# Attention scores in four 64x64 tiles at a time, keys in token order, and a new order of the whole program

## The chip, the cores and the metric

The kernel runs on one core of a Trainium2 chip. The core has five engines that work side by side: TensorE (PE in the profile, its weight loads PEld), VectorE (DVE), ScalarE (ACT), GpSimd (POOL) and SyncE (SP, which here only starts transfers). They share the on-chip memory SBUF; TensorE writes to the eight banks of PSUM. Transfers run on 16 DMA engines. The metric is the time of one execution on the device in microseconds (us).

## What is computed

Cosine attention over 8 batches, 12 heads, 448 tokens and 64 features for each head, and then a highway layer over the 3584 tokens of 768 features:

```python
q_n = q / (np.linalg.norm(q, axis=-1, keepdims=True) + 1e-06)
k_n = k / (np.linalg.norm(k, axis=-1, keepdims=True) + 1e-06)
scores = np.matmul(q_n, k_n.transpose(0, 1, 3, 2)) / tau
attn = np.exp(scores - np.max(scores, axis=-1, keepdims=True))
attn = attn / (np.sum(attn, axis=-1, keepdims=True) + 1e-09)
x = np.matmul(attn, v)                    # then heads side by side: 3584 x 768
H = np.maximum(x @ w_h, 0.0)
T = 1.0 / (1.0 + np.exp(-(x @ w_t + b_t)))
out = T * H + (1.0 - T) * x
```

## The kernel before

**Tokens.** The 448 tokens of a head are read as 64 partitions times 7 pieces: token 7l+j lies in partition l, piece j. Two heads that follow each other lie in the two halves of the partitions (s = 0 and 1), and two such pairs stand side by side (t = 0 and 1). So the program handles "quads" of four heads, three for each batch (g), each of two steps s; a step works on two heads, t = 0 and 1. For each batch there are six steps (p = 0 to 5), 48 in all.

**Stages of a batch.** `ld_qk` and `ld_v` load q, k and v. `norm` squares (ACT, a few on POOL) and sums (DVE, L391), `lnexp` or `newton` turns the sums into reciprocal norms, `scale` multiplies q and k by them (L432, nearly all on POOL), `turn` transposes the result so that features lie on the partitions (PE and a copy by DVE at L462, or a transposing DMA from SP for q from batch 3 and for k from batch 5 on), `scores` makes the products of keys and queries with the keys on the partitions (L496 and L507), ACT takes their exponential into E and Et (L502, L509), `attend` multiplies by v (L521, L526, L534), where a column of ones beside v gives the sum of the row, and DVE divides (L541, L542). Batch 0 does this in smaller pieces in `attend0` (L573 to L629). `ffn` is the highway layer of 112 to 128 tokens at a time, 32 pieces: the transposed x (xT) times w_t and w_h (L682; L679 for the last seventh of the tokens), then bias, tanh, gate and the output on DVE, ACT and POOL (L711 to L762).

**Scores before.** 448 keys are 3 x 128 + 64. For a step, three operations `qk` (L496) each hold two matmuls of 64 x 128 weights, one for each head t in its half of the rows of the array; the two run at the same time. The fourth, `qkt` (L507), takes the last 64 keys of both heads in one matmul of 128 x 128 weights. For it `scale` writes k into eight pieces instead of seven, with zeros where the other head's features stand (L432 in two parts of 4 and 3 pieces; zeros by `zkn`, L281), `turn` transposes eight pieces, and `attend` multiplies Et by two blocks of v at once (L521, 130 columns).

**Order.** Nothing is scheduled while it is built: `ORDER` is a table that says in which order the 1948 operations are issued, `SLOTS` says which buffer each takes; both are written out as numbers. Every engine follows its own queue in that order and waits where data or a buffer is missing. Two rules add waits of their own (the last lines of the kernel): a load of q waits for the ACT operation before it in the order, and a POOL operation waits for the last DVE operation before it where both belong to the kinds in `PORT` (48 such waits).

**Zero products.** 18 + 39 matmuls of a block of zeros (wz, L301 and L305), `WARM` and `NF`, stand between the first real ones. Nothing reads what they make.

Of the kernel before, what the change touches and what calls it, by code (L numbers as in the profile page):

```python
# [20 lines left out]
66 1 67 342 68 0 69 3 72 71 7 70 5 42 61 339 23 19 75 74 64 21 44 52 20 51 22 55 79 9 83 43 2 6 14 13 81 82 73 80 8 85  # L21
86 16 84 15 63 39 341 87 76 88 12 95 96 60 108 25 33 56 31 11 38 24 107 46 89 40 114 113 17 37 109 32 4 90 53 30 111
10 97 18 112 98 93 115 118 110 353 54 116 174 91 137 124 117 94 357 92 29 142 173 175 28 122 105 123 99 340 177 59 119
180 354 121 100 125 120 133 127 128 349 141 126 48 138 26 34 350 154 58 178 347 129 140 153 176 131 578 139 144 143
358 78 134 132 130 106 150 149 45 179 348 155 101 102 343 152 151 156 47 77 186 355 57 359 135 189 181 190 182 192 191
351 360 136 361 50 362 183 146 62 104 103 363 364 145 41 147 36 365 148 184 185 187 27 352 383 198 188 158 162 356 377
378 579 161 165 166 157 35 167 164 159 193 194 163 202 49 382 201 345 168 381 379 169 197 195 196 203 204 209 170 160
206 200 199 212 380 210 171 222 172 346 221 205 384 207 266 234 226 208 267 344 211 224 225 233 223 227 366 367 213
809 214 235 286 271 272 385 368 287 369 370 584 215 371 372 581 592 216 236 228 268 291 217 386 269 238 218 404 585
219 387 245 270 237 273 588 593 248 220 246 229 403 393 240 239 292 430 230 288 247 416 388 242 231 398 293 65 389 432  # L30
241 392 391 394 583 397 289 589 232 243 279 280 413 274 417 431 290 244 427 306 275 281 429 395 428 307 249 415 410
414 316 317 412 250 396 252 390 586 318 594 401 424 253 587 276 580 582 590 402 450 254 376 277 425 311 255 595 312
278 256 808 260 426 259 411 319 451 294 262 591 375 433 261 1263 373 596 434 251 320 374 407 313 597 295 408 263 441
598 264 599 813 409 257 435 600 436 442 308 309 443 437 812 824 816 299 282 601 602 321 265 310 811 438 447 449 258
607 461 448 611 608 444 825 613 634 300 399 301 418 420 463 446 445 462 439 440 467 609 400 421 458 468 464 419 817
631 460 466 405 614 633 465 296 406 297 459 610 612 621 298 818 326 475 617 481 632 476 483 477 455 422 484 423 454
624 327 615 623 616 478 622 469 618 470 819 485 482 501 453 604 479 480 452 502 498 1036 456 302 500 495 619 472 471
487 499 496 492 486 663 488 603 820 620 606 497 605 494 457 473 489 283 637 640 474 490 491 493 814 815 641 505 625
504 503 642 822 638 639 506 643 507 328 508 528 645 329 646 821 509 626 333 334 644 657 647 304 284 303 664 674 330
628 823 335 651 627 648 650 697 680 649 658 566 547 654 826 659 676 681 675 652 660 532 314 827 810 828 829 1038 662  # L40
331 305 830 834 529 315 1037 1039 831 322 332 530 533 832 336 635 531 1035 655 636 843 698 661 513 656 534 1051 514
677 653 1270 671 323 510 511 540 665 337 541 667 678 515 679 629 512 672 673 837 1052 838 666 542 839 842 840 1043 691
685 859 630 855 1044 668 846 847 850 714 518 669 519 520 516 692 715 856 693 683 682 670 848 535 708 688 694 684 537
1271 538 695 1262 689 710 690 686 521 522 539 728 696 687 709 730 705 711 324 841 1045 712 523 567 707 702 713 568 729
833 536 543 1046 569 706 844 1047 701 731 700 338 551 699 732 703 835 851 725 1041 845 722 552 723 724 1048 553 718
559 560 716 717 544 887 726 870 1042 727 1049 889 704 736 719 735 734 890 852 857 733 720 561 721 325 849 285 858 737
556 557 836 860 738 864 872 871 891 888 777 867 861 558 1050 884 570 869 853 885 1274 572 573 886 854 545 865 866 881
898 571 883 1053 739 1054 517 873 758 874 1266 1055 1056 882 862 1057 1058 868 1490 1060 1059 548 863 549 924 900 899
550 892 894 877 876 1067 796 901 904 574 1275 895 878 740 893 1268 1065 1076 546 1087 1264 875 575 879 896 741 903 902
925 524 743 576 907 762 905 1272 526 1278 525 742 897 880 744 770 906 554 918 1279 915 555 908 771 763 916 759 527  # L50
1276 745 1040 1273 1064 760 1073 917 764 1070 1074 748 761 919 920 772 749 1066 1075 932 1082 1505 921 938 751 752 934
933 767 909 940 1083 750 910 941 911 1267 1269 1084 768 958 922 923 939 765 753 1277 935 959 562 769 1062 952 912 1280
766 936 929 797 1068 1063 1078 1489 798 913 914 953 937 746 955 949 577 1069 942 928 951 799 1061 781 782 1281 956 957
773 1265 954 950 563 1071 778 779 1072 926 774 927 1501 780 946 963 783 1111 1108 1282 943 945 1100 944 962 1493 564
# [809 lines left out]
```

## Time and profile before

| what | us |
|---|---|
| median of 3 runs | 255.94 |
| lowest and highest run | 255.06, 262.05 |
| span of the profiled execution, first to last instruction | 252.9 |
| busy in it: PE | 237.5 |
| ACT | 211.5 |
| DVE | 208.0 |
| POOL | 184.0 |

The profile is of one execution and gives its span; a time of the runs also holds what lies around the span, and the profile does not show the device time of that same execution. Between the span and the median of the runs lie 3.0 us. Engines work side by side, so their busy times do not add up. A busy time is that of the union of the instructions; matmuls overlap, and the time from the start of one to the start of the next tells what it costs the queue.

### The profile page before, as it was taken

What the parts mean: (1) busy time and instruction counts of PE and PEld (TensorE: products, weight loads), DVE (VectorE), ACT (ScalarE), POOL (GpSimd) and SP (SyncE); (2) the same over time, 40 slices, a digit from 0 to 9 for tenths busy, and PEclk for the clock granted to TensorE, in tenths of its full rate; (3) what the DMA queues carried; (4) which work ended last, traced back from release to release, by engine and by line L of the source; (5) the groups of instructions that cost most, each with busy time, mean ns of one, the idle gap of its engine ahead of it and who ended that gap; (6) DMA issues with size and microseconds to landing.
All of it is one profiled execution on the core that took longest, in us unless ns stands there. A gap on an engine that the chain in (4) does not pass through costs nothing.

```text
span 252.9 us, 7457 instructions
## 1 busy us (share of the span) xinstructions
PE 237.5 (94%) x2895; PEld 147.1 (58%) x2895; DVE 208.0 (82%) x462; ACT 211.5 (84%) x421; POOL 184.0 (73%) x261
## 2 busy tenths in 40 slices
PE   5959999999999999989999999999999999999990
PEld 2425776557756665645765566656656655675650
DVE  4977989999999999989899869689767665556983
ACT  3589999999999999989999999999997669981120
POOL 8369599959798979796989775878476983522540
PEclk9997999999999999999999999999999999999998
DMA  6999999999589999999999998999779588745755
GB/s 219 286 270 237 288 259 202 200 271 179 72 104 146 314 264 248 151 223 163 266 157 170 156 114 138 249 207 193 128 129 231 93 135 192 162 127 123 187 147 156
DMA packets 75892, 47.78 MB, mean 189 GB/s; under 512 B 51536, under 2 KB 72656, under 8 KB 75856
## 3 DMA queue, kind: packets, MB, share of 16 engines
q1 hardware_dynamic: 55568, 33.86, 59.2%
q0 software_dynamic: 19856, 12.68, 37.1%
q10 hardware_dynamic: 432, 0.75, 0.8%
q8 instruction: 22, 0.36, 0.6%
q14 instruction: 14, 0.11, 0.1%
HBM read 38.34 MB, written 11.01 MB: 195 GB/s over the span
## 4 chain that ended last, share of the span: by engine, by line
PE 68%; DMA 11%; ACT 8%; DVE 7%; issue 2%; POOL 2%; SPq 0%; DVEq 0%; POOLq 0%; ACTq 0%
PE B L682 26%; PE B L496 10%; PE B L526 8%; DMA xT<-x 7%; PE B L679 5%; PE B L521 3%; DMA E<-in_k_dram 3%; PE B L447 3%; ACT E L502 3%; PE B L534 3%; PE B L507 2%; PE B L573 2%; ACT sq L380 2%; PE B L305 2%; DVE hm L720 1%
## 5 line engine op out<-in xcount | busy, mean ns | idle before, releaser
L502 ACT ACTIVATE E<-B 128x448 f16<-128x448 f32 x252 | 122.8, 612 | 9.6 <-PE B L496 8.6
L682 PEld LDWEIGHTS <-xT 128*128 128x128 f16 x576 | 52.1, 98 | 39.6 <-issue 6.9
L752 POOL TENSOR_TENSOR os<-x,hm 128x384 f32<-128x384 f16 x53 | 47.6, 912 | 29.8 <-DVE hm L747 21.3
L682 PE MATMUL B<-wh,xT 128*128 128x384 f16 x288 | 56.7, 326 | 0.6 <-DMA xT<-x 0.6
L682 PE MATMUL B<-wt,xT 128*128 128x384 f16 x288 | 55.0, 326 | 1.8 <-DMA xT<-x 1.4
L432 POOL TENSOR_TENSOR kn<-kr,y 128x192 f16<-128x192 f16 (+1 forms) x84 | 45.8, 562 | 10.6 <-DVE y L409 6.1
L391 DVE TENSOR_REDUCE n<-sq 128x14 f32<-128x896 f32 (+1 forms) x50 | 51.2, 1039 | 2.8 <-ACT sq L380 2.6
L432 POOL TENSOR_TENSOR qn<-qr,y 128x448 f16<-128x448 f32 x47 | 43.9, 946 | 9.1 <-ACT y L420 4.4
L526 PE MATMUL B<-vp,E 128*128 128x65 f16 x756 | 38.7, 193 | 0.0
L724 ACT ACTIVATE tt<-z 128x768 f16<-128x768 f32 (+1 forms) x32 | 26.3, 821 | 14.6 <-DVE z L711 14.5
L720 DVE SCALAR_TENSOR_TENSOR hm<-B,x 128x384 f16<-128x384 f32 x53 | 28.8, 549 | 8.4 <-PE B L682 3.9
L526 PEld LDWEIGHTS <-E 128*128 128x128 f16 x756 | 33.7, 98 | 3.2
L496 PE MATMUL B<-qT,kT 64*128 64x448 f16 x252 | 34.8, 354 | 0.4 <-DVE hm L720 0.4
L711 DVE TENSOR_TENSOR z<-B,bias 128x384 f32<-128x384 f32 x48 | 25.8, 551 | 9.3 <-PE B L682 6.3
L521 PE MATMUL B<-vp,Et 128*128 128x130 f16 x126 | 28.1, 223 | 0.0
L380 ACT ACTIVATE sq<-qr 128x896 f32<-128x896 f32 (+1 forms) x24 | 24.1, 1022 | 3.5 <-DMA qr<-in_q_dram 3.5
L509 ACT ACTIVATE Et<-B 128x448 f16<-128x448 f32 x42 | 26.1, 631 | 0.4 <-PE B L507 0.4
L542 DVE SCALAR_TENSOR_TENSOR x<-B,rd 128x448 f16<-128x448 f32 x42 | 25.6, 618 | 0.9
L337 POOL DMA_DIRECT2D vr<-in_v_dram x32 | 21.9, 690 | 2.5 <-DVE z L711 2.5
L586 ACT ACTIVATE E<-B 128x512 f16<-128x512 f32 (+1 forms) x42 | 20.6, 607 | 0.9 <-POOL qn L432 0.5
L380 ACT ACTIVATE sq<-kr 128x896 f32<-128x896 f16 x17 | 17.0, 1041 | 1.1 <-DMA kr<-in_k_dram 1.1
L305 PE MATMUL B<-wz 128*128 128x512 f16 x39 | 14.7, 433 | 2.6 <-DVE wz L281 2.6
(81 smaller groups left out, 313.7 us busy)
## 6 DMA issues: line engine op xcount, KB each, us to landing
out_dram<-os SPq DMA_DIRECT2D x47, 192.0 KB, 3.3
qr<-in_q_dram SPq DMA_DIRECT2D x6, 1344.0 KB, 8.3
kr<-in_k_dram POOLq DMA_DIRECT2D x7, 672.0 KB, 11.6
vr<-in_v_dram POOLq DMA_DIRECT2D x16, 192.0 KB, 6.9
qr<-in_q_dram SPq DMA_DIRECT2D x6, 448.0 KB, 10.0
vr<-in_v_dram POOLq DMA_DIRECT2D x16, 144.0 KB, 7.7
out_dram<-os SPq DMA_DIRECT2D x15, 96.0 KB, 3.8
wt<-in_moe_w_t_dram POOLq DMA_DIRECT2D x1, 1152.0 KB, 24.4
```

Source lines behind the costliest of these rows:

```text
L380: nc.scalar.activation(dst, src, AF.Square, scale=sc)
L391: nc.vector.reduce_sum(R("n2", b)[:, c : c + 7 * n], a, axis=AX.X)
L432: ENG[eng].tensor_mul(N[:, :, t, :] if nm == "q" else N[:, lo > 0 : (lo > 0) + 2 * (hi - lo) - 1 : 2, t, :], source(nm, b, g)[:, t, 64 * l ...
L496: nc.tensor.matmul(R("B", ("S", n, c, t))[:, 0:S], lhsT=R("kT", i)[ln, s, 128 * c : 128 * c + 128], rhs=queries(ln), start=True, stop=True)
L502: nc.scalar.activation(R("E", n)[:, at : at + 7, :].rearrange("l j x -> l (j x)"), R("B", ("S", n, c, t))[:, 0:S], AF.Exp)
L509: op("ACT", f"expt {n}", lambda: nc.scalar.activation(R("Et", n).rearrange("l j x -> l (j x)"), R("B", ("St", n))[:, 0:S], AF.Exp), r=[("B ...
L521: nc.tensor.matmul(U[:, 2 * c : 2 * c + 2, :], lhsT=Et[:, 2 * c : 2 * c + 2, :].rearrange("l j x -> l (j x)"), rhs=vp[:, 6:8, 0:65], start ...
L526: nc.tensor.matmul(U[:, 2 * c + t, :], lhsT=E[:, at : at + 2, :].rearrange("l j x -> l (j x)"), rhs=vp[:, 3 * t + m, 0:65], start=False, s ...
L682: nc.tensor.matmul(P[:, 0:MH], lhsT=xT[:, cc, :], rhs=w_[:, cc, MH * mh : MH * mh + MH], start=(cc == 0), stop=(cc == CC - 1))
L720: op("DVE", f"hm {g} {mh}", lambda at=at, sl=sl, mh=mh: nc.vector.scalar_tensor_tensor(out=R("hm", g)[:, sl], in0=R("B", at)[:, 0:MH], sca ...
L724: op("ACT", f"th{nb} {g}", lambda: nc.scalar.activation(R("tt", g)[:, 0:W], R("z", g)[:, 0:W], AF.Tanh, scale=0.5), r=[("z", g), ("t0",)], ...
L752: op(eng, f"out {g} {mh}", lambda sl=sl, mh=mh: ENG[eng].tensor_add(R("os", g)[:, sl], xpart(mh), R("hm", g)[:, sl]), r=[("gg", g), xk], w ...
```

## The change

- **Scores in 64x64 tiles.** `score` issues four matmuls of 64 x 64 weights: rows t and columns h of the array are halves, so four tiles. Three operations `qk` for a step take 2 x 64 keys each for two heads, as before. The last 64 keys of the two steps of a quad go together into one operation (`tails`, 21 instead of 42), whose columns h are the two steps. Et then holds both steps in its two halves, one tile for each t, and there are two exponentials for each quad instead of one for each step: 42 as before.
- **k in token order.** k has seven pieces without zeros, like q: `scale` writes it in one operation, `turn` transposes seven pieces, and the transposing DMA is one of 128 partitions instead of two of 64. `zkn` goes. qT and kT have the same layout.
- **Products with v.** The 130 columns of L521 become two matmuls of 65 columns, with zeros in the half of v that belongs to the other step; v is loaded by s instead of by t.
- **Loads.** q is loaded in thirds in all batches (24 transfers instead of 12), and the first k through ACT's queue alone.
- **Batch 0.** q and k of all three quads are scaled half on DVE, half on POOL, instead of that of the first quad alone.
- **Waits.** The two rules go. `BEHIND` is a table of 52 waits: 42 of POOL operations for a DVE operation, 10 of loads of q for an ACT operation.
- **Zero products.** 50 instead of 39 in `NF`, and 18 as before.
- **Order.** `ORDER` and `SLOTS` are new throughout.

```diff
-66 1 67 342 68 0 69 3 72 71 7 70 5 42 61 339 23 19 75 74 64 21 44 52 20 51 22 55 79 9 83 43 2 6 14 13 81 82 73 80 8 85
+74 75 81 4 3 22 0 76 20 82 8 78 5 17 1 9 2 12 77 11 335 19 15 16 10 21 83 18 14 13 80 7 6 23 338 24 87 89 25 26 79 84
...
+BEHIND = dict(
+    map(int, n.split(":"))
+    for n in """
+116:119 136:131 277:589 317:813 332:99 374:358 379:365 547:1250 548:731 564:221 576:275 597:588 732:951 752:1033
...
-    WARM, NF, NLATE = 18, 39, 2
+    WARM, NF, NLATE = 18, 50, 2
...
-    SCALE = {("q", 0, 0): ("DVE", "POOL"), ("k", 0, 0): ("DVE", "POOL")}
+    SCALE = {(nm, 0, g): ("DVE", "POOL") for nm in "qk" for g in range(NG)}
...
+    def score(out, o, w, K, Q, s, c):
+        for t, h in ((0, 0), (1, 1), (0, 1), (1, 0)):
+            ln = slice(64 * t, 64 * t + 64)
+            S_, j = (s, c + h * (4 - s)) if c < NC else (h, 3 + 3 * h)
+            nc.tensor.matmul(out[t][64 * h : 64 * h + 64, o[t] : o[t] + w], lhsT=K[ln, j, S_, :], rhs=Q[ln, :, S_, :], start=True, stop=True)
...
-                for t in range(2):
-                    ln = slice(64 * t, 64 * t + 64)
-                    nc.tensor.matmul(R("B", ("S", n, c, t))[:, 0:S], lhsT=R("kT", i)[ln, s, 128 * c : 128 * c + 128],
-                                     rhs=queries(ln), start=True, stop=True)
-            op("PE", f"qk {n} {c}", fn, r=[tn("q", i), tn("k", i)], w=[("B", ("S", n, c, 0)), ("B", ("S", n, c, 1))], mode="T")
+                score([R("B", ("S", n, c, t)) for t in range(2)], (0, 0), S, R("kT", i), R("qT", i), s, c)
+            op("PE", f"qk {n} {c}", fn, r=[tn("q", i), tn("k", i)], w=[("B", ("S", n, c, 0)), ("B", ("S", n, c, 1))], mode="Q")
...
+    def tails(b, g):
+        i = 3 * b + g
+
         def ft():
-            nc.tensor.matmul(R("B", ("St", n))[:, 0:S], lhsT=R("kT", i)[:, s, 384:512], rhs=queries(slice(0, 128)), start=True, stop=True)
-        op("PE", f"qkt {n}", ft, r=[tn("q", i), tn("k", i)], w=[("B", ("St", n))], mode="F")
+            score([R("B", ("St", i, t)) for t in range(2)], (0, 0), S, R("kT", i), R("qT", i), 0, NC)
+        op("PE", f"qkt {i}", ft, r=[tn("q", i), tn("k", i)], w=[("B", ("St", i, 0)), ("B", ("St", i, 1))], mode="Q")
...
         def full(c):
-            nc.tensor.matmul(U[:, 2 * c : 2 * c + 2, :], lhsT=Et[:, 2 * c : 2 * c + 2, :].rearrange("l j x -> l (j x)"),
-                             rhs=vp[:, 6:8, 0:65], start=True, stop=False)
             for t in range(2):
-                for m in range(NC):
+                for m in range(NC + 1):
+                    lt = E[:, 7 * (2 * m + t) + 2 * c :][:, 0:2] if m < NC else R("Et", (i, t))[:, 2 * c : 2 * c + 2]
+                    nc.tensor.matmul(U[:, 2 * c + t, :], lhsT=lt.rearrange("l j x -> l (j x)"),
+                                     rhs=vp[:, 3 * t + m if m < NC else 6 + t, 0:65], start=(m == 0), stop=(m == NC))
...
-            before = act = None
+            last = {}
...
+                last[o.seq] = made[-1]
+                if o.seq in BEHIND:
+                    behind(made[0], last[BEHIND[o.seq]])
```

What the new order does is best seen in the engines' queues. Rows name the line in the kernel, the instruction, and what it writes and reads. First TensorE in the middle of the program, at the scores of a step. Before, two row pairs of 64x128 tiles and the last keys as one full matmul, and then transposes of k:

```order
L496 LDWEIGHTS kT1_91
L496 MATMUL B3_124<-qT1_87,kT1_91 128x448
L496 LDWEIGHTS kT1_91
L496 MATMUL B5_126<-qT1_87,kT1_91 128x448
L507 LDWEIGHTS kT0_90
L507 MATMUL B0_121<-qT3_89,kT0_90 128x448
L447 LDWEIGHTS kn1_67
L447 MATMUL B7_128<-ident_129,kn1_67 128x2x64
```

And TensorE now, at the last keys of the two steps of a quad, with the highway layer behind them:

```order
L458 LDWEIGHTS kT0_90
L458 MATMUL B7_129<-qT1_87,kT0_90 64x448
L458 LDWEIGHTS kT0_90
L458 MATMUL B4_126<-qT1_87,kT0_90 64x448
L458 LDWEIGHTS kT0_90
L458 MATMUL B7_129<-qT1_87,kT0_90 64x448
L458 LDWEIGHTS kT0_90
L458 MATMUL B4_126<-qT1_87,kT0_90 64x448
L665 LDWEIGHTS xT0_106
L665 MATMUL B3_125<-wt_132,xT0_106 128x384
```

Four matmuls of half the partitions, two into each of two banks, stand where one full matmul stood, once for two steps. Counted along TensorE's whole queue, neighbours with different tiles (128x128, 64x128, 128x64, or now 64x64) follow each other 184 times before and 199 times now.

Second VectorE at the start, in batch 0 (sq, n, y: squares, their sums and the reciprocal norms; kn and qn: scaled k and q of a quad; kT and qT, and for the first quad x: transposed). Before:

```order
L432 TENSOR_TENSOR qn0_83<-qr0_61,y0_78 128x7x64
L281 MEMSET kn0_66 128x32 x2
L391 TENSOR_REDUCE n20_76<-sq0_73 128x14
L432 TENSOR_TENSOR kn0_66<-E0_94,y0_78 128x4x64
L432 TENSOR_TENSOR kn0_66<-E0_94,y0_78 128x3x64
L462 COPY x0_102<-B2_123 128x896
L462 COPY x0_102<-B0_121 128x1024
```

VectorE now, from the same place on:

```order
L432 TENSOR_TENSOR qn0_83<-qr0_61,y0_78 128x7x64
L432 TENSOR_TENSOR kn0_66<-E0_94,y0_78 128x7x64
L393 TENSOR_REDUCE n20_76<-sq2_75 128x14
L393 TENSOR_REDUCE n20_76<-sq0_73 128x14
L451 COPY x0_103<-B3_125 128x896
L451 COPY x0_103<-B5_127 128x896
L393 TENSOR_REDUCE n20_76<-sq2_75 128x14
L393 TENSOR_REDUCE n20_76<-sq1_74 128x14
L432 TENSOR_TENSOR kn1_67<-E1_95,y0_78 128x7x64
L432 TENSOR_TENSOR qn1_84<-qr0_61,y0_78 128x7x64
L432 TENSOR_TENSOR kn2_68<-E2_96,y0_78 128x7x64
L432 TENSOR_TENSOR qn2_85<-qr0_61,y0_78 128x7x64
```

Four more scalings, of the second and third quad, have come to VectorE, ahead of the copies of those quads, and the second sum of squares stands behind the scaling of k instead of ahead of it.

Third GpSimd in the same stretch. Before, the scalings of the first two quads, with k in two parts:

```order
L432 TENSOR_TENSOR qn0_83<-qr0_61,y0_78 128x7x64
L432 TENSOR_TENSOR kn0_66<-E0_94,y0_78 128x4x64
L432 TENSOR_TENSOR kn0_66<-E0_94,y0_78 128x3x64
L432 TENSOR_TENSOR qn1_84<-qr0_61,y0_78 128x7x64
L432 TENSOR_TENSOR kn1_67<-E1_95,y0_78 128x4x64
```

GpSimd now:

```order
L432 TENSOR_TENSOR qn0_83<-qr0_61,y0_78 128x7x64
L432 TENSOR_TENSOR kn0_66<-E0_94,y0_78 128x7x64
L432 TENSOR_TENSOR kn1_67<-E1_95,y0_78 128x7x64
L432 TENSOR_TENSOR qn1_84<-qr0_61,y0_78 128x7x64
L339 DMA vr1_70<-in_v_dram 64x6x192
L344 DMA wh_131<-in_moe_w_h_dram 128x6x768
```

Its first scaling has a wait for VectorE's scaling of k of the same quad. After four scalings it is through with the first two quads, where before it had nine.

More of the change, by code (lines that the diff above doesn't have):

```diff
@@ L780 @@
         else:
-            ld_qk("q", b)
+            for g in range(NG):
+                ld_qk("q", b, [g])
             ld_qk("k", b)
@@ L817 @@
                 made = [i for i in nc.cur_bb.bb.instructions[made:] if i.engine == ENG[o.eng].engine]
-                if o.eng == "ACT":
-                    act = made[-1]
-                elif o.held:
-                    behind(made[0], act)
-                elif o.port and o.eng == "DVE":
-                    before = made[-1]
-                elif o.port and before is not None:
-                    behind(made[0], before)
-                    before = None
+                last[o.seq] = made[-1]
+                if o.seq in BEHIND:
+                    behind(made[0], last[BEHIND[o.seq]])
 _INS = ['q', 'k', 'v', 'tau', 'moe_w_h', 'moe_w_t', 'moe_b_t']
```

210 lines of the change are left out of this document (95 added, 115 removed), and 148 rows, old and new, of tables (BEHIND, ORDER).

## The prediction

> **What bounds the kernel now.** I read the page first: busy times, then the slices.
>
> ```profile
> span 252.9 us, 7457 instructions
> PE 237.5 (94%) x2895; PEld 147.1 (58%) x2895; DVE 208.0 (82%) x462; ACT 211.5 (84%) x421; POOL 184.0 (73%) x261
> ACT  3589999999999999989999999999997669981120
> PEclk9997999999999999999999999999999999999998
> PE 68%; DMA 11%; ACT 8%; DVE 7%; issue 2%; POOL 2%; SPq 0%; DVEq 0%; POOLq 0%; ACTq 0%
> ```
>
> TensorE is busy 94% of the span and holds 68% of the chain that ended last. ACT is full from the fourth slice to the thirtieth, some 160 us, and DVE is close behind. Next the busy time by stretches (columns: stretch, then busy time and instructions of PE, PEld, DVE, ACT, POOL, then clock, DMA share, GB/s):
>
> ```profile
> 20.00:40.00 20.00, 20.00 (x303) 13.65 (x300) 17.87 (x47) 19.11 (x40) 16.64 (x25) 0.93 1.14 259
> 60.00:80.00 20.00, 19.80 (x277) 12.70 (x274) 19.13 (x43) 20.00 (x43) 17.71 (x25) 1.00 0.80 100
> 100.00:120.00 20.00, 18.55 (x214) 10.52 (x211) 18.27 (x41) 18.84 (x38) 16.25 (x24) 1.00 1.17 178
> 140.00:160.00 20.00, 19.43 (x262) 12.77 (x261) 15.99 (x37) 19.40 (x41) 14.92 (x21) 1.00 0.93 126
> 240.00:252.90 12.90, 6.46 (x62) 3.76 (x60) 8.24 (x20) 2.12 (x3) 2.90 (x4) 0.94 0.57 153
> ```
>
> From 20 us to 240 us TensorE hardly pauses: of the eleven stretches of 20 us the worst lacks 1.45 us, the next 0.57. Toward the end ACT falls idle (its last ten slices) and TensorE does not. So the end is set by how soon TensorE can begin dense real work, by what that work costs, and by some 6 us of tail. Last the timeline, at the start:
>
> ```profile
> 2.59 1.04 PE L305 MATMUL B<-wz 128*128 128x512 f16 x2 [2.59 <-DVE wz L281]
> 3.42 1.06 PE L301 MATMUL B<-wz 128*128 128x512 f16 x2
> 19.32 1.03 PE L447 MATMUL B<-ident,kn 128*128 128x128 f16 x8 [2.54 <-POOL kn L432]
> 30.03 0.38 PE L305 MATMUL B<-wz 128*128 128x512 f16 x1
> 0.94 1.15 DVE L281 MEMSET vp<- 128x36 f16 x4 [0.94 <-PEq L845]
> 9.59 1.05 DVE L432 TENSOR_TENSOR qn<-qr,y 128x448 f16<-128x448 f32 x1
> 12.09 0.69 DVE L432 TENSOR_TENSOR kn<-E,y 128x256 f16<-128x256 f32 x2
> 10.10 0.95 ACT L380 ACTIVATE sq<-E 128x896 f32<-128x896 f32 x1 [0.96 <-DMA E<-in_k_dram]
> 12.20 0.32 ACT L417 ACTIVATE tu<-n,eps 128x28 f32<-128x28 f32 x1 [1.15 <-DVE n L391]
> 14.77 0.95 ACT L380 ACTIVATE sq<-kr 128x896 f32<-128x896 f16 x1 [1.15 <-DMA kr<-in_k_dram]
> ```
>
> The last zero product stands at 30.03 us. TensorE then has dense work to the end, so until there its time is mostly waiting, filled with zeros; at 16.8 us the filling was too short, TensorE stood 2.54 us for GpSimd's kn, and the page grants 0.7 of the clock in that slice.
>
> **TensorE's work, part by part.** Prices come from the starts of matmuls that follow each other without a wait, first in the timeline, then in the chain of waits (start, length, what):
>
> ```profile
> 122.97 0.28 PE L534 MATMUL B<-vp,E 128*64 128x65 f16 x6
> 123.09 0.20 PE L534 MATMUL B<-vp,Et 128*64 128x65 f16 x2
> 123.12 0.26 PE L534 MATMUL B<-vp,E 128*64 128x65 f16 x6
> 123.35 0.55 PE L496 MATMUL B<-qT,kT 64*128 64x448 f16 x4
> 123.83 0.23 PE L521 MATMUL B<-vp,Et 128*128 128x130 f16 x1
> 124.34 0.35 PE L507 MATMUL B<-qT,kT 128*128 128x448 f16 x1
> 124.53 0.22 PE L521 MATMUL B<-vp,Et 128*128 128x130 f16 x1
> 124.59 0.35 PE L526 MATMUL B<-vp,E 128*128 128x65 f16 x6
> 124.78 0.22 PE L521 MATMUL B<-vp,Et 128*128 128x130 f16 x1
> ```
>
> ```profile
> 113.58 0.67 PE B L496 x6
> 116.76 0.49 PE B L682 x3
> 118.29 0.98 PE B L679 x12
> 121.13 0.45 PE B L447 x8
> ```
>
> - *A pair of score matmuls.* Two pairs last 0.48 us (123.35 to 123.83), three 0.67, so a pair costs 0.19, as much as one full matmul of 448 columns (124.34 to 124.53). What is left of the 0.48, 0.10, is the change from one kind of tile to another.
> - *A quad, new.* No row shows 64x64 tiles. From below it is 0.19, since 448 columns stream in that time in every row above. From above it is 0.38, if only two of the four run at once. Two row tiles run together (0.19 for a pair), and two column tiles do too: 12 matmuls of L679 last 0.98, 0.163 for a pair, and three of the same width by themselves 0.49, 0.163 each. I take 0.20, near the lower end, because both halves of the arrangement show full overlap and 0.01 allows for two more starts.
> - *Sum of the scores.* Before: 42 steps of three pairs and one full matmul, 168 x 0.19 = 31.9. Now 126 quads and 21 for the last keys, 147 x 0.20 = 29.4. That is -2.5. Batch 0's narrow pieces lose 9 of 21 tail operations and have more starts: -0.2.
> - *Products with v.* L521's 130 columns cost 0.06 (124.53 to 124.59) and six of 65 cost 0.19, 0.032 each. 144 operations now have two of 65 for one of 130: 144 x (0.064 - 0.06) = +0.6.
> - *Transposes of k.* 15 fewer of 0.056 (eight in 0.45): -0.8.
> - *Changes of tile.* 199 for 184 in the queue, 15 x 0.10 = +1.5.
>
> Together -1.4 us. TensorE's work is what the span is made of, so this counts in full where TensorE is what is waited for, and not at all where ACT is. Bounds: -2.9 with quads at 0.19, and +25 with quads at 0.38.
>
> A rule of the Trainium skill speaks against the quads: TensorEngine Tiling (Array Packing), section Restrictions, has column tiling turn off the fast weight load, and by TensorE: Matmul & The Clock Gate, section LDWEIGHTS, 64 columns would then take 53 ns, four of them 0.21 us, longer than the stream. By that the quads would give +0.5 instead of -1.4. The trace does not bear it out for two column tiles.
>
> There, eight matmuls of L534 with eight weight loads of 64 columns are issued in 0.15 us (122.97 to 123.12), 0.019 for a load. Four loads of a quad are 0.08 by that row and lie beside 0.19 of stream.
>
> **The start.** Zeros for the warm-up are written first on VectorE now, ahead of the 1.15 us for v (0.94), so TensorE begins at about 1.4 instead of 2.59. That alone is worth nothing, since only zero products gain. The 11 more zero products (0.22 each by 512 columns at the 0.163 of 384, 2.4) cost nothing while data is what is waited for; if that cover is gone they cost 2.4. What moves the start is when the second and third quad are ready. Before, GpSimd scaled them almost alone. The rows of L432 in the table of groups:
>
> ```profile
> L432 POOL TENSOR_TENSOR qn<-qr,y 128x448 f16<-128x448 f32 x47 | 43.9, 946 | 9.1 <-ACT y L420 4.4 <-DMA out_dram<-os 2.6 <-DVE vp L468 1.5
> L432 POOL TENSOR_TENSOR kn<-kr,y 128x256 f16<-128x256 f16 x42 | 25.4, 612 | 3.8 <-DVE hm L747 2.3 <-DVE y L409 1.2 <-DVE tt L726 0.3
> L432 POOL TENSOR_TENSOR kn<-kr,y 128x192 f16<-128x192 f16 x42 | 21.3, 512 | 6.7 <-DVE y L409 4.8 <-DVE tt L726 1.2 <-DVE hm L747 0.5
> ```
>
> The second quad cost GpSimd 2 x 0.95 + 2 x 0.61 + 2 x 0.51, over 4 us in a row. Now it has one q and one k, and VectorE the others. There a scaling costs between 0.69 (both parts of k, 448 elements, 12.09) and 1.05 (9.59, beside one of GpSimd's); six now for two before, so VectorE gets 2.4 to 4.6 us more before 23 us. ACT has the four squares of the second and third quad in a row and so need not stand idle for its three waits (0.96, 1.15, 1.15 = 3.3) except some 1 us until the first scores: about 2 us sooner. The bounds: at best TensorE never waits, and 1.4 + 68 x 0.22 + 8.3 of real work that the queue holds ahead of the last zero product, by the prices above, + some 1.5 for the slow first ones (two in 0.83, 2.59 to 3.42, where two later ones take 0.43) gives 26.2 instead of 30.2, -4.0; at worst VectorE's extra work is on the path, +2.4. I take -2.0, since ACT is the fullest engine there.
>
> **Transfers.** The chain shows two late xT, where others land in a median of 3.8 us:
>
> ```profile
> xT<-x SPq DMA_TRANSPOSE x28, 3.8
> ```
>
> ```profile
> 100.76 7.62 DMA xT<-x
> 130.47 10.94 DMA xT<-x
> ```
>
> They stand in the stretches that lack 1.45 and 0.57 us. Thirds of q let a transpose pass between them, but the same bytes move, and their issue costs SP, which computes nothing. Between 0 and -2.0 us; -0.4, since nothing shows which load held them up.
>
> **What costs nothing.** GpSimd's k goes from 612 + 512 ns to one scaling of 912 (the line through both rows at 448 elements) to 946 (q's row), in all some 12 us less of 184; it is on 2% of the chain, so ACT and TensorE hide that. Its waits are 42 for 48. The copies of k on VectorE shrink by an eighth. Twelve more issues on SP and two on ACT lie beside the first loads. The tail has the same operations in nearly the same order: 0.
>
> **Sum.** 252.9 - 1.4 - 2.0 - 0.4 = 249.1 of span. The median of the runs lies 3.0 above the span, and I keep that: 252.1 us.
>
> **Rivals.**
> - *ACT takes the gain.* ACT's exponentials and squares are the same in number, and in the stretch 60 to 80 it was busy all 20.00 us. If the start is not sooner for ACT, what TensorE saves becomes waits for exponentials, and the time stays at 255.9 (254.5 to 257.5). Against it: the last 30 us, and the idle 3.3 us of ACT at the start.
> - *Everything fits.* Quads at 0.19 (1.5 more), the start at its bound (2.0 more), no late xT (1.6 more): 247.0, and anything from there to 250.8. For it: TensorE already ran stretches without a gap, so a new order can do without the others.
> - *Quads do not run four abreast.* At 0.38 it is 147 x 0.18 = +26 on the forecast, 278 us; if the four loads of 0.019 show each time, 147 x 0.08 = +12, 264. The break-even with before is 0.20 + 3.8/147 = 0.23 for a quad, and it is slower by 2% from 0.26. For it: no row has four tiles. Against it: the rows of L496, L679 and L534. I give loads that show 0.04 and two passes 0.05.
> - The Trainium skill's page TensorEngine Tiling (Array Packing), Restrictions, names a cause for loads that show; by the figure worked out above the time would be 254.0, within the 2%.
> - *GpSimd's waits stall the scaling.* Some 15 of the 42 hold a scaling for a VectorE operation that it does not need. Waits of that kind cost GpSimd 2.8 us in 4 cases before (kn for hm), 0.7 each. If 15 such lie on the path to scores, +10.5, 262.6; it is slower than before from 6 on. Against it: GpSimd is busy 73% and has 12 us less to do.
>
> ```profile
> POOL kn L432 <- DVE hm L747: 2.8, 4, 0.9
> ```
>
> **How the numbers follow.** Forecast 0.41; ACT takes the gain 0.18; everything fits 0.28; quads not abreast 0.09; waits 0.04. About 2% is what a measurement of this kernel can tell from no change, 5.1 us. Faster by more is under 250.8: the third case, 0.28. Slower by more is above 261.1: the last two, 0.13. Within it 0.59. The likeliest case alone spans 250.8 to 254.5; the range of 8 in 10 takes in the case of ACT and all of the third case, and leaves out the last two: 247.0 to 258.5.
>
> **What would show it.** Right: one quad start to the next 0.19 to 0.21 us within an operation's run; the last zero product ends before 29 us; no stop of 2.5 us ahead of the second k transposes and no slice of low clock after the first; ACT full from the third or fourth slice on; GpSimd's busy time near 172. Wrong: quads at 0.25 or more; stretches of 20 us after the start in which TensorE lacks more than the 1.45 us of before, released by ACT's exponentials or by kn; a last zero product at 31 us or later.

## The result and the profile after

The changed kernel takes 256.51 us on the median of 20 runs (254.63 to 257.93), the kernel before 255.8 on the median of 20 runs beside it. The ratio of their times is 1.008, with a 95% interval of 1.0051 to 1.011: slower by 1.3 to 2.8 us, where a gain of 3.8 was forecast. It is less than the 2% that decides, and it has the other sign. The ratio, here and below, counts only fast runs, those within 1.5% of the fastest of their kernel (here 11 of the 20 before and all 20 after), so it is not the quotient of the medians.

First the changed kernel's page: span, busy times, the slices of ACT and of the granted clock, and the engines' shares of the chain that ended last.

```profile
span 255.5 us, 8673 instructions
PE 238.1 (93%) x3497; PEld 147.6 (58%) x3497; DVE 209.4 (82%) x459; ACT 211.3 (83%) x421; POOL 172.6 (68%) x210
ACT  3496899999999699999999999999978779971220
PEclk9999799999999999999999999999999999999995
PE 58%; DMA 15%; ACT 9%; POOL 5%; DVE 4%; issue 4%; SPq 2%; DVEq 0%; POOLq 0%; ACTq 0%
```

TensorE has lost ten points of the chain, and transfers have gained four. The slice of low clock has not gone: it was the fourth, it is now the fifth (25.6 to 31.9 us), still at 0.7. Before, it was the slice behind the stop of 16.8 to 19.3 us, rather than the slice in which that stop began; now it follows a stop too (below). The last zero product stands at 32.06 us, past the 31 that the prediction had named as a sign of being wrong. GpSimd's busy time is 172.6 us, near the 172 of the forecast, yet its part of the chain has grown from 2 to 5%. Then the stretches (stretch, then busy time and instructions of PE, PEld, DVE, ACT, POOL, then clock, DMA share, GB/s):

```profile
20.00:40.00 20.00, 16.99 (x365) 11.56 (x369) 15.18 (x41) 16.51 (x34) 9.21 (x13) 0.91 1.13 271
80.00:100.00 20.00, 18.61 (x266) 11.02 (x264) 17.04 (x34) 18.06 (x37) 16.34 (x19) 1.00 1.21 250
160.00:180.00 20.00, 18.77 (x276) 11.89 (x276) 17.21 (x34) 18.55 (x38) 15.09 (x19) 1.00 1.20 217
```

The stretch from 20 to 40 us, full before, now lacks 3.01 us of TensorE and has ACT at 16.51 for 19.11. The timeline shows the start (PE: zero products at L307; ACT: the squares at L382):

```profile
17.49 0.55 PE L448 MATMUL B<-ident,kn 128*128 128x128 f16 x7 [0.43 <-DVE kn L432]
24.22 0.38 PE L307 MATMUL B<-wz 128*128 128x512 f16 x1 [2.25 <-ACT E L574]
32.06 0.39 PE L307 MATMUL B<-wz 128*128 128x512 f16 x1
5.45 0.58 ACT L382 ACTIVATE sq<-qr 128x448 f32<-128x448 f32 x1 [2.89 <-DMA qr<-in_q_dram]
5.46 0.37 ACTq L330 DMA_DIRECT2D E<-in_k_dram  x1
8.94 0.95 ACT L382 ACTIVATE sq<-E 128x896 f32<-128x896 f32 x1
9.80 0.93 ACT L382 ACTIVATE sq<-qr 128x896 f32<-128x896 f32 x1
12.70 0.95 ACT L382 ACTIVATE sq<-E 128x896 f32<-128x896 f32 x1 [1.97 <-DMA E<-in_k_dram]
13.55 0.93 ACT L382 ACTIVATE sq<-qr 128x896 f32<-128x896 f32 x1
14.39 0.30 ACT L419 ACTIVATE tu<-n,eps 128x28 f32<-128x28 f32 x1
22.73 0.95 ACT L382 ACTIVATE sq<-qr 128x896 f32<-128x896 f32 x1 [2.16 <-DMA qr<-in_q_dram]
```

The stop of 2.54 us ahead of the second k transposes is 0.43 now. In its place a zero product stands 2.25 us at 24.22, for a PSUM bank that ACT's exponential has not read yet, and ACT is late because at 22.73 it has stood 2.16 us for a square of q. Ten microseconds earlier it stood 1.97 us for a k. That k was sent for only at 5.46, since its load stands on ACT's queue behind the first square. The chain of waits of this kernel names the same k; these are its second and third piece (start, length, what):

```profile
0.74 4.69 DMA qr<-in_q_dram
5.46 7.22 DMA E<-in_k_dram
```

The q is not on that chain, which runs from 16.60 to 23.59 us over VectorE and GpSimd. For the second wait, so far, the timeline alone speaks, and GpSimd's row of scalings and issued loads is a rival there, until the experiments.

Last the ends of TensorE's work, first in the kernel before, then in the changed one:

```profile
245.28 1.18 PE L695 MATMUL B<-wh,xT 128*64 128x192 f16 x24
```

```profile
246.74 1.16 PE L678 MATMUL B<-wh,xT 128*64 128x192 f16 x24
```

That divides the span's 2.6 us. Up to the start of the last zero product it is 30.03 before and 32.06 after, +2.03. From there to the end of the last matmul (246.46 and 247.90) it is 216.43 and 215.84, -0.59. From there to the end of the span it is 6.4 and 7.6, +1.2. How TensorE spends the middle part, the stretch table tells for just these windows:

```profile
30.03:246.46 216.43, 213.13 (x2671) 133.55 (x2667) 182.33 (x402) 190.54 (x384) 164.67 (x228) 1.00 0.98 180
```

```profile
32.06:247.90 215.84, 211.18 (x3159) 133.16 (x3152) 183.62 (x402) 189.96 (x383) 154.33 (x182) 1.00 1.02 178
```

It is busy 1.95 us less in the changed kernel and idle for 4.66 us, where it was 3.30, +1.36. One execution's span is no median: for these two profiled executions the spans differ by more than the medians do (2.6 for 0.7), so the parts are read for their places rather than to the tenth.

### The profile page after: what moved, and what is told of

Its sections match the earlier page's. It is cut to its first block, busy times and chain, and to the rows that moved or that the text cites. A ratio compares the mean times of both kernels' runs of the same rounds, so it can differ in the third digit from the quotient of the medians.

```text
span 255.5 us, 8673 instructions
## 1 busy us (share of the span) xinstructions
PE 238.1 (93%) x3497; PEld 147.6 (58%) x3497; DVE 209.4 (82%) x459; ACT 211.3 (83%) x421; POOL 172.6 (68%) x210
## 4 chain that ended last, share of the span: by engine, by line
PE 58%; DMA 15%; ACT 9%; POOL 5%; DVE 4%; issue 4%; SPq 2%; DVEq 0%; POOLq 0%; ACTq 0%
PE B L665 22%; PE B L458 12%; PE B L516 11%; ACT E L488 6%; DMA qr<-in_q_dram 5%; PE B L662 4%; DMA kT<-kn 3%; DMA E<-in_k_dram 3%; DMA out_dram<-os 3%; PE B L524 2%; PE B L448 2%; PE B L588 2%; DMA qT<-qn 2%; ACT sq L382 2%; POOL os L735 1%
## 5 line engine op out<-in xcount | busy, mean ns | idle before, releaser
L432 POOL TENSOR_TENSOR qn<-qr,y 128x448 f16<-128x448 f32 x45 | 41.7, 935 | 14.3 <-PE B L458 6.5
L458 PE MATMUL B<-qT,kT 64*64 64x448 f16 (+2 forms) x812 | 48.1, 323 | 2.5 <-ACT E L488 0.8
L432 POOL TENSOR_TENSOR kn<-kr,y 128x448 f16<-128x448 f16 x42 | 38.8, 935 | 16.0 <-DVE y L411 9.6
L516 PEld LDWEIGHTS <-E 128*128 128x128 f16 x756 | 35.0, 97 | 8.1 <-issue 4.0
L516 PE MATMUL B<-vp,Et 128*128 128x65 f16 x252 | 35.2, 191 | 0.0
L694 DVE TENSOR_TENSOR z<-B,bias 128x384 f32<-128x384 f32 x48 | 25.6, 550 | 8.2 <-PE B L665 8.1
L458 PEld LDWEIGHTS <-kT 64*64 64x64 f16 x812 | 18.4, 106 | 21.4 <-issue 14.5
L382 ACT ACTIVATE sq<-qr 128x896 f32<-128x896 f32 (+1 forms) x24 | 24.5, 1021 | 6.6 <-DMA qr<-in_q_dram 6.6
L516 PEld LDWEIGHTS <-Et 128*128 128x128 f16 x252 | 24.8, 99 | 0.0
L499 ACT ACTIVATE Et<-B 128x448 f16<-128x448 f32 x42 | 24.2, 620 | 0.1
L574 ACT ACTIVATE E<-B 128x384 f16<-128x384 f32 (+2 forms) x42 | 19.9, 584 | 1.6 <-PE B L588 1.2
## 6 DMA issues: line engine op xcount, KB each, us to landing
wt<-in_moe_w_t_dram POOLq DMA_DIRECT2D x1, 1152.0 KB, 22.1
```

The costliest lines, as they stand in the source:

```text
L382: nc.scalar.activation(dst, src, AF.Square, scale=sc)
L432: ENG[eng].tensor_mul(R(nm + "n", i)[:, :, t, :], source(nm, b, g)[:, t].rearrange("l (j d) -> l j d", d=D), R("y", b)[:, c : c + NJ].unsq ...
L458: nc.tensor.matmul(out[t][64 * h : 64 * h + 64, o[t] : o[t] + w], lhsT=K[ln, j, S_, :], rhs=Q[ln, :, S_, :], start=True, stop=True)
L516: nc.tensor.matmul(U[:, 2 * c + t, :], lhsT=lt.rearrange("l j x -> l (j x)"), rhs=vp[:, 3 * t + m if m < NC else 6 + t, 0:65], start=(m == ...
L694: op("DVE", f"za {g} {mh}", lambda at=at, sl=sl: nc.vector.tensor_add(R("z", g)[:, sl], R("B", at)[:, 0:MH], biast[:, :] if tail else bias ...
```

## The experiments

Three theories stood at first. LOADS: the start is late because ACT comes, in its fixed order, to data that were sent for too late. ZEROS: the zero products in that stretch hold TensorE, since each takes a bank and 0.22 us. LATER: the start does get sooner, but what it gains is lost again behind 40 us. All ratios are to the kernel before, on the same chip; the experiments ran on three chips, so a ratio compared with one from another chip is a weaker comparison.

**One load on another queue.** The third quad's k goes through SP's queue, where it does not stand behind ACT's first square.

```diff
-                    ld_kf(g, "ACT")
+                    ld_kf(g, "SP" if g == 2 else "ACT")
```

> The changed kernel with one edit: the first k of the third quad is loaded through SP's queue, behind the three loads of q, instead of through ACT's behind its first square. Theory LOADS (the start was lost where ACT, in its fixed order, waits for data that was sent for late: 1.97 us for this k, 2.16 us for the second batch's q): ACT's wait of 1.97 us at 10.7 goes, the second k transposes on TensorE start near 15.5 instead of 17.49, the last zero product about 1.5 us sooner than 32.06 unless the second wait takes it back, ratio to before 1.001 to 1.006 instead of 1.008. Rival ZEROS (the 11 more zero products and the bank that one of them waits for hold TensorE back): the last zero product stays at 32, ratio 1.008. Rival LATER (the start does get sooner, but ACT or transfers take it back after 40 us): last zero product near 30.5 and ratio 1.007 to 1.009.

255.78 us, ratio 1.0063 (1.0024 to 1.0103). ACT's wait for k fell from 1.97 to 1.25 us, where LOADS had it go, and the next one stayed:

```profile
12.05 0.95 ACT L382 ACTIVATE sq<-E 128x896 f32<-128x896 f32 x1 [1.25 <-DMA E<-in_k_dram]
22.42 0.95 ACT L382 ACTIVATE sq<-qr 128x896 f32<-128x896 f32 x1 [2.30 <-DMA qr<-in_q_dram]
```

What ACT won at 12 us it lost again at 22.4, because that q lands when it lands. The last zero product stands at 31.90, for 32.06; alone this run tells LOADS from ZEROS by no more than a ratio whose interval holds both.

**One load released.** The second batch's first q was held on SP's queue until ACT's square of the first batch's third quad of q. Now it waits for an earlier square (93), and the load after it is held in its place.

```diff
-... 332:99 ...
+... 332:93 333:99 ...
```

> The changed kernel with one edit in the table of waits: the first third of the second batch's q no longer waits for ACT's square of the third quad (14.5 us) but for its second square (6 us); the next third waits where the first one did. Theory LOADS: ACT's wait of 2.16 us at 20.6 goes, with it the zero product that stands 2.25 us for a bank of PSUM, the clock of the slice stays near full, the last zero product is about 2 us sooner than 32.06, ratio 0.999 to 1.003. A loss would come from the third quad's k landing later than 12.70. Rival ZEROS: the wait for the bank stays, ratio 1.008. Rival LATER: last zero product near 30 and ratio 1.007 to 1.009.

253.81 us, ratio 0.9999 (0.9959 to 1.0038). Both waits of the later place are gone, ACT's and the zero product's, and the last zero product starts at 29.59, though GpSimd's queue is as it was. ACT's wait for k has even grown, with one more transfer beside it:

```profile
13.64 0.95 ACT L382 ACTIVATE sq<-E 128x896 f32<-128x896 f32 x1 [2.61 <-DMA E<-in_k_dram]
21.40 0.96 ACT L382 ACTIVATE sq<-qr 128x896 f32<-128x896 f32 x1
```

The slice of low clock is gone with the stop of 2.25 us, which also counts: four zero products in a row that take 1.87 us at 25.70 in the changed kernel take 1.03 at 24.38 here. First the changed kernel's, then this one's, and this one's slices:

```profile
25.70 1.87 PE L307 MATMUL B<-wz 128*128 128x512 f16 x4 [0.25 <-DVE qT L451]
```

```profile
24.38 1.03 PE L307 MATMUL B<-wz 128*128 128x512 f16 x4 [0.43 <-DVE qT L451]
PEclk9999999999999999999999999999999999999995
```

**Both.**

> The changed kernel with both edits. Theory LOADS: both waits of ACT go, 4.1 us in all, last zero product at 28 to 29 us as the prediction had it, ratio 0.992 to 0.997. Rival ZEROS: no change, 1.008. Rival LATER: last zero product at 28 to 29, ratio 1.004 or more, with new gaps of TensorE after 40 us.

253.48 us, ratio 0.9926 (0.9876 to 0.9976): below the kernel before. The first edit is worth 0.0017 alone and 0.0073 on top of the second, but both differences lie within the intervals. The last zero product shows the order of things better: 32.06 with neither, 31.90 with the first, 29.59 with the second and 28.26 with both, so that the first moves it by 0.16 alone and by 1.33 on top of the second. What the first wait gives up, the second takes, until it goes too.

**Fewer zero products.** The last nine are left out, among them the one that waited for a bank. Nothing reads them.

```diff
-lambda i=i: nc.tensor.matmul(
+lambda i=i: i < 41 and nc.tensor.matmul(
```

> The changed kernel without its last nine zero products, those from 21.6 us on; everything else as it is. Nothing reads what they make. Theory LOADS: ACT still waits 2.16 us for the load of q; TensorE's transposes of the third quad's q start 2.3 us sooner, but ACT, which is full from there, hardly gains: ratio 1.004 to 1.009. Rival ZEROS: the 2.25 us and the 1.9 us of work go, ratio 0.993 to 1.000. Loss possible through the clock, if TensorE then idles: up to 1.012.

255.84 us, ratio 1.008 (1.0038 to 1.0121), the same as with them. ZEROS falls; what waited behind the zero product waits without it as well (TensorE stands 2.56 us for ACT's exponential ahead of 25.04).

**The reverse, in the kernel before.** The same load (339 there) is moved behind the same square (91), and so held for it; nothing else is changed.

```diff
-... 42 61 339 23 ... 174 91 137 ...
+... 42 61 23 ... 174 91 339 137 ...
```

> The kernel before with one load moved: the second batch's first q is held on SP's queue until ScalarE's square of the first batch's third quad of q, as the changed kernel holds it. LOADS (whichever order of products stands around it, ScalarE comes to that q too early and TensorE runs dry behind it): time rises by 1 to 2.5 us, ratio 1.004 to 1.010, and ScalarE shows a wait for that q of 1 us or more. CHANGED START ALONE (the load was late only beside the changed kernel's other order, where zero products were moved up): within 0.5 us of the kernel before, since that q is read there later.

262.5 us, ratio 1.024 (1.0184 to 1.0296), from six runs. That is more than was expected of it, and clearly slower, though not clearly by 2%. ACT's wait is longer than the changed kernel's, and the last zero product comes at 34.71 for 30.03:

```profile
24.85 0.95 ACT L379 ACTIVATE sq<-qr 128x896 f32<-128x896 f32 x1 [5.69 <-DMA qr<-in_q_dram]
```

ACT comes to that q at 19.2 us (24.85 - 5.69) and finds it at 24.85; in the changed kernel it comes at 20.6 and finds it at 22.73. So the late load slows either kernel, and the changed one less, which has its square of the third quad sooner and other work for ACT first.

**All loads of batch 0 as before.** k of the second and third quad (77, 79) go on SP's queue ahead of the third quad's q (78), and the second batch's first q is released as above.

```diff
-... 0 76 20 82 8 78 ... 12 77 11 ... 26 79 84 ...
+... 0 76 77 79 20 82 8 78 ... 12 11 ... 26 84 ...
-                    ld_kf(g, "SP" if g == 2 else "ACT")
+                    ld_kf(g, "SP" if g else "ACT")
```

> The changed kernel with all of batch 0's loads as the kernel before sends them (k of the 2nd and 3rd quad on SP's queue, both ahead of the third quad's q) and the second batch's first q released at once. LOADS (the start is set by when these loads land, in ScalarE's order): no more than the two load edits gave, 253 to 254 on the median, ratio 0.990 to 0.996, last zero product before 29 us; ScalarE's wait for the third quad's k under 1 us. ORDER (the changed kernel's later order of squares wants q of the third quad first, so that k ahead of it on the queue only swaps one wait for another): ratio 0.997 to 1.004, with a wait of 1 us or more for that q.

253.04 us, ratio 0.9876 (0.9806 to 0.9947), last zero product at 28.08, where the forecast of 2.0 us less than before gives 28.03. As ORDER said, ACT has a wait of over 1 us for the third quad's q (1.17), but the median is that of LOADS and the ratio a little below its range: the row of waits is short enough now. TensorE's waits have a new line here (total, times, longest); of the kernels above only the one with both edits has it, with 1.7 us:

```profile
PE B L663 <- DMA wt<-in_moe_w_t_dram: 1.6, 1, 1.6
```

With the attention's start 4 us sooner, the highway layer's first product comes to gate weights that have not landed: they are sent at 6.05 us on GpSimd's queue and land 28.3 us later. In the changed kernel the same transfer, sent at the same time, took 22.1; with the other loads sent sooner it lands later.

So a part of the gain is lost again, as LATER had it, some of it already before 40 us. Behind the last zero product TensorE is idle 6.93 us in this kernel, for 4.66 in the changed one; of the 4.0 us that the start gains, 2.3 turn into waits, these 1.6 among them.

```profile
28.08:246.24 218.16, 211.23 (x3159) 132.97 (x3152) 183.04 (x402) 190.46 (x383) 155.20 (x182) 1.00 1.02 179
```

**Those weights sooner.** They (84) go ahead of a slice of the second batch's v (338).

```diff
-... 23 338 24 87 89 25 26 84 ...
+... 23 24 87 89 25 26 84 338 ...
```

> The changed kernel with all the load edits (loads of batch 0 as the kernel before sends them, second batch's first q at once) and the gate weights sent on GpSimd's queue ahead of the second batch's last slice of v (144 KB), which stood ahead of them. With the load edits alone TensorE waited 1.63 us at 32.8 us for those weights, which landed 28.3 us after their issue. WEIGHTS (the start's gain runs into the next load): that wait falls to under 0.9 us, ratio 0.983 to 0.990. OTHER (the pace of all transfers sets it, since 16 engines were busy throughout, or the next wait takes it): the wait stays over 1.2 us or the ratio stays at 0.988 to 0.997.

253.26 us, ratio 0.9925 (0.9881 to 0.9968). The wait is gone, as WEIGHTS had it, and the ratio is that of OTHER. This is TensorE behind the highway layer's first product, at 33.15, in this kernel:

```profile
33.15 0.65 PE L663 MATMUL B<-wt,xT 128*128 128x384 f16 x3
33.73 0.35 PE L456 MATMUL B<-qT,kT 64*64 64x128 f16 x9
34.97 0.25 PE L456 MATMUL B<-qT,kT 64*64 64x128 f16 x4 [0.89 <-issue]
```

The product no longer waits, and the scores behind it stop for 0.89 us. The three kernels with the loads mended (0.9926, 0.9876, 0.9925) can't be told apart by these intervals; all three lie below the kernel before.

**The tail.** The last group's gate products and its sums were put earlier in the order, since in the changed kernel VectorE ends as one row without a gap, in which an operation beside GpSimd's last takes nearly twice its time:

```profile
246.60 1.78 POOL L735 TENSOR_TENSOR os<-x,hm 128x384 f32<-128x384 f16 x2 [2.47 <-DVE hm L730]
247.78 1.01 DVE L700 TENSOR_TENSOR os<-hm,os 128x384 f32<-128x384 f16 x1
248.88 0.55 DVE L700 TENSOR_TENSOR os<-hm,os 128x384 f32<-128x384 f16 x1
```

> The changed kernel with its last stretch in another order: the last group's two gate products stand ahead of the group before it's second pair of products, and its bias sum, its tanh and the product of group 29 move up with them on VectorE and ScalarE. TAIL (the changed kernel lost 1.2 us behind the zero products because VectorE has the last group's bias sum at 247.31 us, three microseconds later than the kernel before, and ends as a row of operations without a gap): time 0.7 to 1.5 us under the changed kernel's 256.5, ratio to the kernel before 1.003 to 1.006, distance from TensorE's last product to the end of the span under 7 us. REST (what follows the last product is set by the stores, and the order of the sums ahead of them is worth nothing): 256.2 to 256.8, ratio 1.007 to 1.010.

256.39 us, ratio 1.0112 (1.0079 to 1.0144). TAIL's ratio was missed. In the profile the distance from the last product to the end fell from 7.6 to 6.7 us, as expected, but no time follows it. The same edit on top of the mended loads, on two chips:

> The changed kernel with the third quad's k sent on SP's queue, the second batch's first q released at once, and the last stretch in the other order. LOADS AND TAIL add: 3.0 us from the loads (253.5 was had with both) and 0.7 to 1.5 from the tail: 252.0 to 252.8, ratio 0.987 to 0.990, which is the forecast that the prediction made. If the tail is worth nothing: 253.5, ratio 0.993. If the start's gain is swallowed later: above 254.

253.2 us, ratio 0.9961 (0.993 to 0.9991), where 0.9926 was had without it on another chip.

> The same with the last stretch in the other order (last group's gate products ahead). TAIL (the profile had 7.6 us from TensorE's last product to the span's end in the changed kernel, 6.7 in the one with this order): 0.5 to 1.0 us under the kernel beside it on the same chip, a ratio lower by 0.002 to 0.004. NOTHING: the two within 0.3 us.

253.79 us, ratio 0.9898 (0.982 to 0.9976), beside 0.9876 on the same chip. Three times no gain, though only the last pair ran side by side on one chip. And the distance is no property of the order: with the tail as it was, it is 6.8 us in the kernel with the loads as before (253.0 of span, last product ended at 246.2) and 6.9 in the one with the weights sooner. What makes it 7.6 in the changed kernel's profiled execution stays open.

**GpSimd's waits.** The changed kernel's table holds 57 waits, 45 of GpSimd operations for VectorE and 12 of loads of q for ACT; the 52, 42 and 10 given ahead of the prediction are miscounted. Here it is without the 45:

```diff
-116:119 136:131 277:589 ... 332:99 ...
+332:99 ...   (the loads of q alone)
```

> The changed kernel without any of the waits that hold a GpSimd operation behind one of VectorE (they only order, no data depends on them); the loads stay held. WAITS STALL (a GpSimd operation that waits delays those behind it, the rival of the prediction): time falls by 1 us or more, to 255.5 or under. WAITS HELP (they keep VectorE's operations of two 16-bit inputs off the shared port's lock): time rises by 0.5 us or more, scalings by VectorE in the first 20 us go from 0.62 back to about 1.05 us. NEITHER: 256.0 to 257.0.

282.21 us, ratio 1.107 (1.1005 to 1.1135). WAITS HELP has the direction, and not the size: some 25 us of loss, by the two ratios, where 0.5 us or more was expected. VectorE's groups in the changed kernel and then in this one (busy us, mean ns of one; then idle time before them):

```profile
L730 DVE TENSOR_TENSOR hm<-tt,hm 128x768 f16<-128x768 f16 x23 | 14.8, 641 | 0.2
L709 DVE TENSOR_SCALAR tt<-tt 128x768 f16<-128x768 f16 x24 | 11.4, 477 | 0.7 <-ACT tt L707 0.7
L407 DVE TENSOR_TENSOR tu<-y 128x84 f32<-128x84 f32 x12 | 2.9, 245 | 0.1
L432 DVE TENSOR_TENSOR kn<-E,y 128x448 f16<-128x448 f32 x3 | 2.1, 685 | 0.0
```

```profile
L726 DVE TENSOR_TENSOR hm<-tt,hm 128x768 f16<-128x768 f16 x23 | 18.0, 784 | 0.2
L705 DVE TENSOR_SCALAR tt<-tt 128x768 f16<-128x768 f16 x24 | 17.2, 720 | 0.2
L403 DVE TENSOR_TENSOR tu<-y 128x84 f32<-128x84 f32 x12 | 5.7, 479 | 0.1
L428 DVE TENSOR_TENSOR kn<-E,y 128x448 f16<-128x448 f32 x3 | 4.3, 1442 | 0.0
```

The four groups take 14.0 us more, in the steps that lead from squares to norms and from gate to output, and TensorE waits behind them: its stretch from 140 to 160 us has 15.05 us of work, from 80 to 100 it has 16.50 (19.64 and 18.61 with the waits), at a granted clock of 0.83 and 0.91 for 1.00, and VectorE's share of the chain is 13%, for 4. The Trainium skill (SBUF — State Buffer, section SBUF: two separate sides) has the two engines share a pair of ports under a lock that the first holds for its whole instruction. The trace agrees for these groups; the reciprocals that VectorE takes from PSUM (L531 in the changed kernel) last 199 ns with the waits and 195 without.

The kernel before has 48 such waits, set by a rule. Without them:

```diff
-                elif o.port and before is not None:
-                    behind(made[0], before)
-                    before = None
```

> The kernel before without its waits of GpSimd operations behind VectorE (it sets them by a rule, the changed kernel by a list; the changed kernel lost 24 us without them). REPLACED (both kernels live by such waits, so that the list only replaces the rule and the change's term for it is near 0): slower by 3% or more. NEW (the order of the changed kernel alone needs them): within 1% of the kernel before.

279.01 us, ratio 1.0876 (1.0731 to 1.1022). REPLACED: both kernels live by them. The ratio rests on four runs. The two gate groups lengthen there too, from 592 to 832 ns and from 430 to 585.

## Why the prediction was wrong

**TensorE's work, -1.4: right in its price for a quad.** A quad was priced at 0.20 with bounds of 0.19 and 0.38. In the changed kernel's chain of waits three quads and one change of tile take 0.69, and in its timeline two quads and a change take 0.50, from the first start to that of the operation behind:

```profile
149.43 0.69 PE B L458 x12
```

```profile
86.65 0.57 PE L458 MATMUL B<-qT,kT 64*64 64x448 f16 x8
87.15 0.66 PE L665 MATMUL B<-wh,xT 128*128 128x384 f16 x3
```

So the third quad costs 0.19, which leaves 0.12 for the change; with the prediction's 0.10 for a change, a quad of these two costs 0.20. All four tiles run at once and their four weight loads are hidden; the rival in which they are not is out. The Trainium skill (TensorE: Matmul & The Clock Gate, section LDWEIGHTS) gives 0.21 us for four loads of 64 columns, as an estimate, and a quad that had to wait for them could not take less; the 0.19 of the third quad does. The total of -1.4 was not measured by itself: the 1.95 us that TensorE is busy less behind the last zero product also holds what the new order does ahead of it.

**The start, -2.0: wrong, it measured +2.0.** The step that failed is the sentence that ACT "has the four squares of the second and third quad in a row and so need not stand idle for its three waits". The prediction looked at which squares stand in a row and not at when their data are sent for. The row holds: 8.94, 9.80, 12.70 and 13.55 us. In the middle of it ACT stands 1.97 us for a k that its own queue sent late, so the second quad's norms, which now stand behind the third quad's k, come at 14.39 instead of 12.20. A second wait of 2.16 us at 22.73 is for a load that the table of waits holds. Both stood in the list of the change ("the first k through ACT's queue alone", which means that of batch 0 in all three quads; and the loads of q behind ACT). The k was costed as two more issues that "lie beside the first loads"; the held q had no term at all. Mending both loads moves the last zero product to 28.08, and the ratio from 1.008 to between 0.988 and 0.993. That is shown. That the start then agrees with the forecast's -2.0 is partly luck, since ACT still has a wait of 1.17 us in its row. The bound of +2.4 for the start's worst case came from VectorE's extra scalings; the size was about right, the cause was not: those of the second and third quad took 0.83, 0.61, 0.61 and 0.61 us from 16.52 on, and they stand unchanged in the kernels with the loads mended, whose start is 4 us sooner.

**Late xT, -0.4: there, and replaced.** Matmuls waited 2.0 us (2 waits) for a transposed x before and 0.8 (1) after. But the stretches of 80 to 100 and 160 to 180 us lack 1.39 and 1.23 where before two others lacked 1.45 and 0.57: TensorE's idle time behind the last zero product is 1.36 us more, which takes back most of the 1.95 that its work there is shorter. Three of its waits there are for ACT's exponentials (0.43, 0.52 and 0.82 us, where before had two of 0.2), three for transposing transfers of x, k and q (0.82, 0.77 and 0.71). Which of the new order's pairs of neighbours cause them was not tried.

**The tail, 0: mis-sized by 1.2 in the profile.** No experiment turned that into time.

**GpSimd, 0: right in sum.** The rival that its waits stall the scaling is out, by the kernel without them. The count of waits fell from 48 to 45, not to 42. The rival's counter-argument, that GpSimd is 73% busy and has less to do, was beside the point: what the waits are worth is on VectorE.

**The sum.** The start came 4.0 us later than forecast; behind it TensorE's work is 1.95 us less and its waits 1.36 more, and 1.2 at the tail was not forecast: 2.03 - 1.95 + 1.36 + 1.2 = 2.6, the span's difference. The rival "ACT takes the gain" came nearest, at 255.9, and had the right engine: ACT was not sooner. That its number fits is luck: its reason was exponentials in a full ACT, and at the start ACT was idle. Its wait for exponentials is there behind the start, 1.8 us in all.

**Span and median.** The 3.0 us between the two were kept for the changed kernel. There the distance is 1.0 (256.51 and 255.5). In every run whose own span is on record the time lies 1.72 to 1.85 above it; the rest is which execution was profiled, a short one before and a long one here. So the term was too large by about 1.2.

## What to carry to other kernels

When an order is changed, follow each load from where it is issued, on which queue and behind which instruction, to the first engine that reads it; a load that an engine issues itself, behind an instruction that waits, goes out late: the k here at 5.46 us, behind a square that had waited 2.89. Two waits on one engine's queue can hide each other, as the 0.16 and 1.33 us of the same edit show: try them together. A gain at one place can turn into a wait at the next, so measure that too. And a wait that only orders may be what keeps another engine fast; take it out by experiment before calling it a cost.

## What the runs showed beside

- Without the waits of GpSimd for VectorE, either kernel loses a tenth or nearly so (ratios 1.107 and 1.0876), although GpSimd's busy time hardly changes (176.3 for 172.6 us).
- A gain at the start runs into the next load: with ACT's waits gone, the highway layer's first product stood 1.6 us for weights sent at 6 us, which landed after 28.3 us instead of 22.1.
- Four matmuls of 64x64 tiles and 448 columns cost what one full matmul of 448 does, 0.19 to 0.20 us, with four weight loads hidden beside them.
